# One Mish of 2048 columns per tile in place of an Exp-Ln-Exp chain per step, while attention runs

## Chip, core and metric

The kernel runs on one core of one Trainium2 chip. The metric is the device time of one launch in microseconds (us), as the median of several runs. A difference below 0.5% of this kernel's time (5.6 us) is called no change.

## What is computed

Causal attention with a decay, then two feed-forward layers on its output, all in float32:

```python
# B, H, S, D = 4, 8, 576, 64
scores = scale * np.matmul(q, k.transpose(0, 1, 3, 2))
decay = cum[:, :, :, None] - cum[:, :, None, :]
scores = np.where(causal, -1000000000.0, scores + decay)
attn = softmax(scores)                       # over the last axis
x = heads_joined(np.matmul(attn, v))         # 2304 tokens x 512
h = x @ w_in                                 # layer 1: 512 -> 2048
g = h * np.tanh(np.log1p(np.exp(h)))         # Mish
x = g @ w_out                                # 2048 -> 512
h = x @ moe2_w_in; g = h * np.cos(h); out = g @ moe2_w_out   # layer 2
```

## The kernel before

**Number format.** Matrix products run in float32r. To keep the accuracy every operand is split into a high and a low part (`gh`/`gl`, `wih`/`wil`, `woh`/`wol`), and a product is three matmuls: high times high, high times low, low times high.

**Attention** works on one pair of heads of one batch at a time, query block by query block (names `stk`, `s`, `mx`, `sm`, `p`, `xs`). PE makes the scores (L524), DVE adds the mask and takes the maximum (L560), ACT does the Exp (L565), DVE and POOL normalise (L576 to L579), PE transposes the probabilities (L606, L622), ACT and DVE copy them out of PSUM (L598, L600), and PE multiplies with v (L644). ACT and DVE split the result (L659, L660), and SP stores it to `xd` in DRAM.

**Layer 1 beside attention.** The first half of layer 1 (chunks 0 to 3 of eight, the "lo" weights) is done in tiles of 256 tokens. A tile is four steps of 512 columns: two blocks of 128 hidden units times 256 tokens, in one PSUM bank `h`. A step is 24 matmuls that make `h` (`mm_h`, L208), an activation, and 24 matmuls that bring the result back to 512 features in `acc` (`mm_o`, L230). Tiles are read from `xd` into `xa`. A tile is available when the whole batch that holds its last token is done, so layer 1 runs behind attention by about a batch, and its units are taken one by one between the pieces of attention, by a credit that is topped up at each piece. Tile 5 is held back (`LATE_TILES`) for the end of attention. `ffn_units` keeps three steps (`LAG = 3`) between the matmuls that make `h` and those that use the activated result.

**The activation** of a first-layer step is computed in two ways. When attention is over it is one ACTIVATE with the function Mish (L287). While attention runs, ACT uses a table of functions that holds Exp and Ln but not Mish, and the step is a chain: ACT Exp (L291), DVE twice (L302, L303), ACT Ln and Exp (L316, L317), DVE four times (L327 to L330, the last of which reads `h` from PSUM once more), ACT copy to `gh` (L338), POOL subtraction to `gl` (L344):

```python
nc.scalar.activation(out=e, in_=t, func=AF.Ln, bias=two)
nc.scalar.activation(out=e, in_=e, func=AF.Exp, scale=-1.0)
...
if n in hps and steps[n][1]["layer"] == 1:
    nc.gpsimd.tensor_tensor(out=gl, in0=st[n][0], in1=f(gst[n][0]), op=ALU.subtract)
```

**After attention** its PSUM banks and its SBUF pools (`att`) are given up, and new pools (`late`, `w1`) take their place. The rest of layer 1 follows (the other half of the weights, "hi", is first converted from a 64-bit layout by DVE, ACT and POOL, names `raw`, L123 to L138), then layer 2.

**Order.** The program is written unit by unit, and a scheduler then sets the order of the instructions on each engine. On the chip each engine works its list in that order.

Of the kernel before, what the change touches and what calls it, by code (L numbers as in the profile page):

```python
# [17 lines left out]
MISH_CAP = 485165195.40979  # L18
INV_2PI = 0.15915494309189535
TWO_PI = 6.283185307179586  # L20
ROUND = 12582912.0
# [15 lines left out]
def tile_attention_two_ffn(  # L37
# [35 lines left out]
    two = const.tile([128, 1], F32, name="two")  # L73
# [70 lines left out]
    def ffn_units(passes, p, hbank, abank, ready):  # L144
# [44 lines left out]
        def tmp(tag, n, dt=F32, bufs=3):  # L189
            tl = steps[n][1]  # L190
            t = p.tile([128, 512], dt, tag=tag, name=tag, bufs=bufs)
            return t[:, 0 : tl["G"] * tl["T"]]
# [103 lines left out]
        def v_1(n):  # L296
# [3 lines left out]
            t = tmp("n", n, F32, 2)  # L300
            if steps[n][1]["layer"] == 1:
                nc.vector.tensor_scalar(out=t, in0=e, scalar1=MISH_CAP, scalar2=2.0, op0=ALU.min, op1=ALU.add)  # L302
                marks["v1"] = nc.vector.scalar_tensor_tensor(  # L303
                    out=t, in0=e, scalar=MISH_CAP, in1=t, op0=ALU.min, op1=ALU.mult
                )
            else:
                nc.vector.tensor_scalar(out=t, in0=e, scalar1=ROUND, scalar2=ROUND, op0=ALU.add, op1=ALU.subtract)
                marks["v1"] = nc.vector.tensor_tensor(out=t, in0=e, in1=t, op=ALU.subtract)  # L308
            st[n].append(t)

        def a_mid(n):
            if n not in hps:
                return
            e, t = st[n]
            if steps[n][1]["layer"] == 1:
                nc.scalar.activation(out=e, in_=t, func=AF.Ln, bias=two)  # L316
                nc.scalar.activation(out=e, in_=e, func=AF.Exp, scale=-1.0)  # L317
            else:
                nc.scalar.activation(out=t, in_=t, func=AF.Sin, scale=TWO_PI)  # L319

        def v_2(n):
            e = st[n][0]
            if n in hps:
                t = st[n][1]
                if steps[n][1]["layer"] == 1:
                    r = tmp("r", n, F32, 1)
                    nc.vector.scalar_tensor_tensor(out=r, in0=t, scalar=2.0, in1=e, op0=ALU.add, op1=ALU.mult)  # L327
                    nc.vector.scalar_tensor_tensor(out=r, in0=r, scalar=2.0, in1=e, op0=ALU.subtract, op1=ALU.mult)
                    nc.vector.tensor_tensor(out=t, in0=t, in1=r, op=ALU.mult)
                    nc.vector.scalar_tensor_tensor(  # L330
                        out=e, in0=t, scalar=-UNSCALE, in1=hps[n], op0=ALU.mult, op1=ALU.mult
                    )
                else:
                    nc.vector.scalar_tensor_tensor(  # L334
                        out=e, in0=t, scalar=UNSCALE, in1=hps[n], op0=ALU.mult, op1=ALU.mult
                    )
# [4 lines left out]
        def v_3(n):  # L341
            gl = tmp("gl", n, F32R)
            if n in hps and steps[n][1]["layer"] == 1:
                nc.gpsimd.tensor_tensor(out=gl, in0=st[n][0], in1=f(gst[n][0]), op=ALU.subtract)  # L344
            else:
                marks["v1"] = nc.vector.tensor_tensor(out=gl, in0=st[n][0], in1=f(gst[n][0]), op=ALU.subtract)  # L346
# [3 lines left out]

        LAG = 3
        ok = lambda i: 0 <= i < N
        for m in range(N + LAG):
            if ok(m) and steps[m][3] == 0:
                while not ready(steps[m][0], steps[m][1]):
# [522 lines left out]
```

## Time and profile before

| what | value |
|---|---|
| median of 3 runs | 1125.5 us (1121.8 to 1126.73) |
| profiled execution | 1120.98 us, span 1119.2 us |
| PE busy | 1057.8 us, 95% |
| DVE busy | 692.5 us, 62% |
| ACT busy | 584.4 us, 52% |
| POOL busy | 274.3 us, 25% |
| attention's last matmuls, on the chain that ended last | 416.64 us, for 2.26 us |

Busy times are of one execution, from its first instruction. Up to about 60 us attention runs alone, from there to 420 us attention and the first tiles of layer 1 share the engines, and the rest is feed-forward work only. An engine that is idle costs time only where the others wait for it.

### The profile page before, as it was taken

To read this page: it belongs to the slowest core of one execution; us is meant where nothing else is said; L and a number is where in the kernel's file an instruction comes from. 1 tells how busy PE (TensorE), PEld (TensorE's weight loads), DVE (VectorE), ACT (ScalarE), POOL (GpSimd) and SP (SyncE) were. 2 spreads that over 40 slices of the span, in tenths; PEclk is the share of its full clock that TensorE was granted. 3 is DMA by queue.
4 is the path that set the end of the run, shared out by engine and by line. 5 is a ranking of instruction groups with operands and counts; after the bars stand their busy time and mean duration, and the time that the engine had idled before them with its cause. 6 is when DMAs were issued, how large, how long until landed. Compare 5 with 4: busy or idle time off the path is not lost.

```text
span 1119.2 us, 18191 instructions
## 1 busy us (share of the span) xinstructions
PE 1057.8 (95%) x6496; PEld 949.3 (85%) x6496; DVE 692.5 (62%) x1597; ACT 584.4 (52%) x1261; POOL 274.3 (25%) x365
## 2 busy tenths in 40 slices
PE   4688899889999999999999999999999999999998
PEld 3467688568877879999999999879999999999997
DVE  6888897668866764573456433996545454454543
ACT  5666777767765764454344433564434343343433
POOL 5557664434433421341111100231000000000000
PEclk9888999989998999999999999999999999999999
DMA  4635542251234102773555652641002020100000
GB/s 105 170 105 139 145 146 74 55 156 35 71 106 135 49 25 81 264 247 99 174 194 168 202 165 86 206 152 57 29 1 85 1 85 1 57 29 1 29 1 29
DMA packets 119503, 110.76 MB, mean 99 GB/s; under 512 B 65173, under 2 KB 101573, under 8 KB 119413
## 3 DMA queue, kind: packets, MB, share of 16 engines
q1 hardware_dynamic: 119412, 109.61, 31.8%
q8 instruction: 51, 0.84, 0.3%
q14 instruction: 40, 0.32, 0.1%
HBM read 81.12 MB, written 28.46 MB: 98 GB/s over the span
## 4 chain that ended last, share of the span: by engine, by line
PE 75%; DVE 10%; DMA 5%; issue 4%; ACT 4%; POOL 2%; SPq 1%; ACTq 0%; DVEq 0%; POOLq 0%
PE h L208 18%; PE acc L239 17%; PE acc L230 14%; PE hx L208 13%; PE s L644 4%; PE s L622 4%; PE s L524 3%; DMA raw<-in_moe_w_out_dram 3%; DVE s L560 2%; DVE stk L502 1%; DVE raw L133 1%; DVE raw L124 1%; PE s L482 1%; DMA xd<-xs 1%; ACT s L565 1%
## 5 line engine op out<-in xcount | busy, mean ns | idle before, releaser
L346 DVE TENSOR_TENSOR gl<-e,gh 128x384 fp32r<-128x384 f32 (+1 forms) x157 | 108.9, 695 | 131.7 <-ACT gh L338 131.0
L208 PE MATMUL hx<-x,wih 128*128 128x384 f32 (+1 forms) x640 | 160.3, 330 | 0.0
L208 PE MATMUL h<-x,wih 128*128 128x384 f32 (+1 forms) x640 | 158.6, 330 | 0.0
L338 ACT ACTIVATE gh<-e 128x384 fp32r<-128x384 f32 (+1 forms) x180 | 97.9, 545 | 101.4 <-DVE e L334 53.8
L230 PE MATMUL acc<-gh,woh 128*128 128x256 f32 (+1 forms) x480 | 147.5, 310 | 2.2 <-ACT part L267 1.7
L230 PE MATMUL acc<-gl,woh 128*128 128x256 f32 (+1 forms) x480 | 147.6, 308 | 0.9 <-POOL gl L344 0.9
L230 PE MATMUL acc<-gh,wol 128*128 128x256 f32 (+1 forms) x480 | 147.2, 307 | 0.0
L524 PE MATMUL s<-stk 68*128 68x192 f32 (+13 forms) x384 | 90.6, 343 | 31.7 <-DVE stk L502 19.0
L208 PEld LDWEIGHTS hx<-x,wih 128*128 128x128 f32 x640 | 115.1, 188 | 4.2
L208 PEld LDWEIGHTS h<-x,wih 128*128 128x128 f32 x640 | 115.1, 188 | 4.0
L579 POOL TENSOR_SCALAR s<-s,sm 128x448 f32<-128x448 f32 (+5 forms) x144 | 90.6, 642 | 108.4 <-DVE sm L577 59.3
L239 PE MATMUL acc<-woh,gl 128*128 128x512 f32 x288 | 113.3, 397 | 3.1 <-DVE gl L346 3.1
L239 PE MATMUL acc<-wol,gh 128*128 128x512 f32 x288 | 113.7, 395 | 0.0
L239 PE MATMUL acc<-woh,gh 128*128 128x512 f32 x288 | 112.3, 390 | 0.9 <-DVE part L275 0.9
L208 PE MATMUL h<-x,wil 128*128 128x384 f32 (+1 forms) x320 | 105.9, 331 | 0.0
L208 PE MATMUL hx<-x,wil 128*128 128x384 f32 (+1 forms) x320 | 105.8, 331 | 0.0
L524 PEld LDWEIGHTS s<-stk 128*128 128x128 f32 (+1 forms) x384 | 61.8, 206 | 44.6 <-DVE stk L502 15.6
L565 ACT ACTIVATE s<-s,mx 128x448 f32<-128x448 f32 (+5 forms) x144 | 83.3, 579 | 30.2 <-DVE mx L560 26.0
L319 ACT ACTIVATE n<-n 128x384 f32<-128x384 f32 x96 | 50.2, 523 | 92.4 <-DVE n L308 92.4
L230 PEld LDWEIGHTS acc<-gh,woh 128*128 128x128 f32 x480 | 91.7, 192 | 4.2 <-ACT part L267 2.2
L230 PEld LDWEIGHTS acc<-gl,woh 128*128 128x128 f32 x480 | 92.4, 193 | 1.5 <-POOL gl L344 1.1
L230 PEld LDWEIGHTS acc<-gh,wol 128*128 128x128 f32 x480 | 92.4, 193 | 0.1
(94 smaller groups left out, 2085.1 us busy)
## 6 DMA issues: line engine op xcount, KB each, us to landing
raw<-in_moe_w_in_dram SPq DMA_DIRECT2D x32, 512.0 KB
raw<-in_moe_w_out_dram SPq DMA_DIRECT2D x32, 512.0 KB
x<-xd SPq DMA_DIRECT2D x6, 1536.0 KB
x<-yd SPq DMA_DIRECT2D x6, 1536.0 KB
xd<-xs SPq DMA_DIRECT2D x12, 576.0 KB
xa<-xd SPq DMA_DIRECT2D x6, 1024.0 KB
natk<-in_k_dram SPq DMA_DIRECT2D x32, 144.0 KB
pd<-part SPq DMA_DIRECT2D x18, 256.0 KB
```

The costliest lines, as they stand in the source:

```text
L208: nc.tensor.matmul(o, lhsT=a[wsl], rhs=b[:, kk, :], start=(kk == 0 and i == 0), stop=(kk == NK - 1 and i == 2),)
L230: nc.tensor.matmul(o, lhsT=a[dsl], rhs=b[:, gs], start=(start and i == 0 and d % nsub == 0), stop=(end and i == 2), skip_group_check=True,)
L239: nc.tensor.matmul(acc[ti][m], lhsT=a[:, ms], rhs=b[:, j, :], start=(start and i == 0), stop=(end and i == 2),)
L319: nc.scalar.activation(out=t, in_=t, func=AF.Sin, scale=TWO_PI)
L338: nc.scalar.activation(out=gh, in_=e, func=AF.Copy)
L346: marks["v1"] = nc.vector.tensor_tensor(out=gl, in0=st[n][0], in1=f(gst[n][0]), op=ALU.subtract)
L524: marks["score"] = nc.tensor.matmul(o, lhsT=wide(st, rows, x, j, cols), rhs=st[rows, 1, x, j, c0:c1], start=x == 0, stop=x == 1,)
L560: marks["ttr"] = nc.vector.tensor_tensor_reduce(out=s[rs, c0:c1], in0=o[rs], in1=mk[rs], scale=-1.0, scalar=BIG if prev is None else prev, ...
L565: nc.scalar.activation(out=s[:, 0:w], in_=s[:, 0:w], func=AF.Exp, scale=-1.0, bias=mx, accum_out=sm[:, j : j + 1])
L579: nc.gpsimd.tensor_scalar(out=s[:, 0:w], in0=s[:, 0:w], scalar1=sm[:, j : j + 1], scalar2=1.0, op0=ALU.mult, op1=ALU.mult)
L622: nc.tensor.transpose(t[:, 128 * x : 128 * x + 128], ss[j][:, QS[c] : QS[c] + 128], ident)
L644: nc.tensor.matmul(t[64 * j : 64 * j + 64, c0:width], lhsT=vt[jb][0:kr, c, j], rhs=pt[0:kr, j, c, c0:width], start=(c == 0), stop=(c == nb ...
```

## The change

The chain is gone. While attention runs, layer 1 is now written by a generator `early()` that works tile by tile: it issues the 8 units of `mm_h` of a tile, and DVE copies each full bank of `h` out of PSUM with the scale applied, into one tile `hb` of 2048 columns. After the last of them one Mish of 2048 columns runs over `hb`, four ACT copies make the high part `ghb`, and four DVE subtractions the low part `glb`. The `mm_o` units of a tile come after the first three `mm_h` units of the next tile, if that one is available, and at once if not. `hb`, `ghb` and `glb` have one buffer each, in attention's SBUF pool. When attention is over, the `mm_o` units that are left are written out before the pools are closed, and the old generator goes on with the next tile (tile 6), whose input is now loaded into the `late` pool. The temporary tiles of the old generator move to that pool as well.

```diff
         def activate(n):
-            first_layer = steps[n][1]["layer"] == 1
             e = tmp("e", n)
-            if first_layer and attention_over:
+            if steps[n][1]["layer"] == 1:
                 nc.scalar.activation(out=e, in_=hps.pop(n), func=AF.Mish, scale=UNSCALE)
-                st[n] = [e]
-                return
-            if first_layer:
-                nc.scalar.activation(out=e, in_=hps[n], func=AF.Exp, scale=UNSCALE)
...
         def v_3(n):
             gl = tmp("gl", n, F32R)
-            if n in hps and steps[n][1]["layer"] == 1:
-                nc.gpsimd.tensor_tensor(out=gl, in0=st[n][0], in1=f(gst[n][0]), op=ALU.subtract)
-            else:
-                marks["v1"] = nc.vector.tensor_tensor(out=gl, in0=st[n][0], in1=f(gst[n][0]), op=ALU.subtract)
+            marks["v1"] = nc.vector.tensor_tensor(out=gl, in0=st[n][0], in1=f(gst[n][0]), op=ALU.subtract)
...
+        def early():
...
+                todo = [("o", n, jj) for n in own[prev] for jj in range(G)] if prev is not None else []
+                if go:
+                    todo[0:0] = [("h",) + u for u in units[0:3]]
+                    for x, u in enumerate(units[3:]):
+                        todo.insert(4 + 2 * x if prev is not None else 3 + x, ("h",) + u)
+                for kind, n, jj in todo:
+                    if kind == "h":
...
+                            nc.vector.tensor_scalar(
+                                out=parts[n - own[ti][0]], in0=hps.pop(n), scalar1=UNSCALE, scalar2=None, op0=ALU.mult
+                            )
...
+                if go:
+                    nc.scalar.activation(out=whole, in_=whole, func=AF.Mish)
...
+                        nc.scalar.activation(out=gh[:, sl], in_=parts[i], func=AF.Copy)
+                        nc.vector.tensor_tensor(out=gl[:, sl], in0=parts[i], in1=f(gh[:, sl]), op=ALU.subtract)
...
+    attention_done = True
+    while next(ffn) != "over":
+        pass
     att_ps.close()
     att_sb.close()
```

Three places of the program show how the instructions stand now. Lines of the changed kernel have other numbers: L551 scores, L592 Exp, L606 normalisation, L625 copies of p, L649 transposes, L671 products with v, L686 copy to xs, L206 `mm_h`, L228 `mm_o`, L366 Mish, L371 `ghb`, L168 loads of x.

ACT at tile 4, with all of the tile's `h` made in the rows before:

```order
L625 ACTIVATE p<-s_4384 128x2x2x128
L592 ACTIVATE s,sm<-s,mx 128x576
L366 ACT_TABLE_LOAD
L366 ACTIVATE hb<-hb 128x2048
L592 ACT_TABLE_LOAD
L592 ACTIVATE s,sm<-s,mx 128x64
```

The load of the functions' table stands ahead of the Mish, and a second one ahead of the next Exp. ACT has 13 such loads in the changed program, and 3 in the one before.

PE at the same place, from the row behind the last `mm_h` matmul of tile 4:

```order
L551 MATMUL s_4395<-stk_99 128x64
L649 MATMUL s_4418<-ident,s 128x128 x3
L649 MATMUL s_4423<-ident,s 128x128 x3
L551 MATMUL s_4432<-stk_99 128x192 x4
L671 MATMUL s_4445<-p,natv 64x320
L649 MATMUL s_4456<-ident,s 128x128 x4
L671 MATMUL s_4445<-p,natv 64x320
L671 MATMUL s_4445<-p,natv 64x256 x2
L671 MATMUL s_4445<-p,natv 64x128 x2
L649 MATMUL s_4462<-ident,s 128x128 x4
L551 MATMUL s_4486<-stk_99 128x320 x2
L551 MATMUL s_4489<-stk_99 128x320 x2
```

All of this is attention's. The scores `s_4489` are written into the bank from which ACT copies `s_4456` to p, and wait for that copy; ACT does it after the Mish, the second load and three Exps. Behind them come four transposes and tile 4's first `mm_o`.

ACT at the end of attention, where tile 5 has its Mish:

```order
L625 ACTIVATE p<-s_5031 128x4x128
L625 ACTIVATE p<-s_5037 128x4x128
L366 ACT_TABLE_LOAD
L366 ACTIVATE hb<-hb 128x2048
L686 ACTIVATE xs<-s_5008 128x320
L625 ACTIVATE p<-s_5068 128x4x128
L625 ACTIVATE p<-s_5074 128x4x128
L625 ACTIVATE p<-s_5080 128x2x128
L371 ACTIVATE ghb<-hb 128x512 x4
L686 ACTIVATE xs<-s_5097 128x256
```

The last three copies of p, for which attention's last products with v wait, stand behind the Mish. On PE those products come next, and after them all 96 `mm_o` matmuls of tile 5, with nothing else between; then the `mm_h` of tile 6.

SP at the hand-over, before (tile 6 is loaded into `xa`; names in brackets are the semaphores that an issue waits for):

```order
L664 DMA xd<-xs 256x1x576 [waits DMAHW6_49,DVE_49]
L170 DMA xa<-xd 128x8x256 [waits DMAHW6_49,DMAHW7_49,DMAHW5_49,DMAHW2_49]
L270 DMA pd<-part_5682 128x2x256 [waits DMAHW0_49,Activation_49]
L270 DMA pd<-part_5685 128x2x256 [waits DMAHW1_49,Activation_49]
L104 DMA raw<-in_moe_w_out_dram 128x1024 [waits DMAHW7_49,PE_49,Pool_49]
```

and in the changed kernel (tile 6 is loaded into `x`):

```order
L691 DMA xd<-xs 256x1x576 [waits DMAHW6_49,DVE_49]
L268 DMA pd<-part_5262 128x2x256 [waits DMAHW7_49,Activation_49]
L168 DMA x<-xd 128x8x256 [waits DMAHW2_49,DMAHW1_49,DMAHW5_49,DMAHW0_49,DMAHW6_49,PE_49,Pool_49]
L268 DMA pd<-part_5265 128x2x256 [waits Activation_49]
L102 DMA raw<-in_moe_w_out_dram 128x1024
```

The load of tile 6 now waits for PE, with the count of the last of tile 5's 96 `mm_o` matmuls; before it waited for other DMAs alone. The first load of a raw weight into the `late` pool waited for PE (the last `mm_h` of tile 6) before, and does no more.

## Rows read from the trace of the kernel before

**Rows 1.** The page's list of engines: busy us, share of the span, instructions.
```profile
PE 1057.8 (95%) x6496; PEld 949.3 (85%) x6496; DVE 692.5 (62%) x1597; ACT 584.4 (52%) x1261; POOL 274.3 (25%) x365
```

**Rows 2.** By stretch: length, PE, PEld, DVE, ACT, POOL busy, granted clock, DMA share, GB/s.
```profile
60.00:195.00 135.00, 122.52 (x921) 102.29 (x920) 114.37 (x316) 94.70 (x229) 82.01 (x106) 0.96 0.45 124
195.00:240.00 45.00, 39.89 (x250) 27.61 (x248) 28.18 (x113) 30.76 (x88) 18.20 (x37) 0.89 0.42 118
240.00:322.00 82.00, 79.99 (x626) 70.14 (x625) 63.75 (x182) 54.85 (x133) 35.47 (x52) 0.98 0.24 62
322.00:346.00 24.00, 21.73 (x134) 15.97 (x133) 13.01 (x48) 15.48 (x41) 7.43 (x15) 0.86 0.59 173
346.00:420.00 74.00, 71.90 (x552) 60.66 (x551) 54.18 (x158) 50.46 (x122) 28.52 (x41) 0.98 0.14 44
...
480.00:500.00 20.00, 18.23 (x134) 17.82 (x133) 15.42 (x21) 11.67 (x21) 8.40 (x6) 0.91 0.61 192
```

**Rows 3.** What PE waited for from 60 to 195 us: total us, times, longest.
```profile
PE s L622 <- DVE mx L560: 3.4, 4, 1.6
PE s L524 <- DVE mx L560: 1.7, 2, 1.3
...
PE acc L230 <- POOL gl L344: 0.9, 1, 0.9
```

**Rows 4.** All instructions on tile n, 60 to 430 us, by engine (DVE, then ACT).
```profile
60.00:430.00 370.00, 79.84 (x115) 16.57 (x23) 0.95 0.35 98
```

**Rows 5.** The chain's other groups, one shape each: count, busy us, mean ns, idle before.
```profile
L344 POOL TENSOR_TENSOR gl<-e,gh 128x512 fp32r<-128x512 f32 x23 | 31.1, 1351 | 29.2 <-ACT gh L338 28.5 <-POOL stk L508 0.7
...
L328 DVE SCALAR_TENSOR_TENSOR r<-r,e 128x512 f32<-128x512 f32 x23 | 17.2, 747 | 0.2
...
L317 ACT ACTIVATE e<-e 128x512 f32<-128x512 f32 x23 | 14.4, 625 | 0.3
...
L291 ACT ACTIVATE e<-h 128x512 f32<-128x512 f32 x23 | 13.6, 592 | 3.9 <-PE h L208 3.7
```

**Rows 6.** The same view: groups that are like what is added or stands near it.
```profile
L598 ACT ACTIVATE p<-s 128x512 f32<-128x512 f32 x80 | 46.2, 591 | 14.5 <-PE s L622 12.2 <-PE s L524 1.6
...
L338 ACT ACTIVATE gh<-e 128x512 fp32r<-128x512 f32 x36 | 22.5, 628 | 10.4 <-DVE e L330 5.1 <-PE acc L230 3.6 <-PE s L622 1.6
...
L287 ACT ACTIVATE e<-h 128x384 f32<-128x384 f32 x24 | 11.7, 486 | 14.0 <-PE h L208 13.8
...
L346 DVE TENSOR_TENSOR gl<-e,gh 128x512 fp32r<-128x512 f32 x13 | 11.4, 873 | 14.5 <-ACT gh L338 14.5
...
L565 ACT ACTIVATE s<-s,mx 128x192 f32<-128x192 f32 x24 | 10.7, 445 | 5.3 <-DVE mx L560 5.3
...
L287 ACT ACTIVATE e<-h 128x512 f32<-128x512 f32 x7 | 4.2, 597 | 1.5 <-PE h L208 1.5
...
L256 DVE TENSOR_SCALAR part<-acc 128x512 f32<-128x512 f32 x6 | 4.1, 684 | 3.9 <-PE acc L239 3.9
```

**Rows 7.** ACT's timeline at the first Mish: start us, us, instruction, idle before and its end.
```profile
425.57 1.28 ACT L287 ACT_TABLE_LOAD   x1 [0.28 <-PE h L208]
426.86 0.60 ACT L287 ACTIVATE e<-h 128x512 f32<-128x512 f32 x1
```

**Rows 8.** The chain that ended last, at the end of attention: start us, us, what.
```profile
412.40 1.24 PE s L622 x10
...
416.64 2.26 PE s L644 x18
...
423.13 5.34 DMA xa<-xd
428.47 0.14 issue
428.60 3.09 PE hx L208 x24
```

**Rows 9.** The same chain, 447 to 500 us, where the second half's weights are converted.
```profile
450.55 7.70 DMA raw<-in_moe_w_out_dram
```

More of the change, by code (lines that the diff above doesn't have):

```diff
@@ L72, in tile_attention_two_ffn @@
     maskt = const.tile([128, S], F32, name="maskt")
-    two = const.tile([128, 1], F32, name="two")
     quarter = const.tile([128, 1], F32, name="quarter")
@@ L190, in tmp @@
             tl = steps[n][1]
-            t = p.tile([128, 512], dt, tag=tag, name=tag, bufs=bufs)
+            t = late[0].tile([128, 512], dt, tag=tag, name=tag, bufs=bufs)
             return t[:, 0 : tl["G"] * tl["T"]]
@@ L299, in v_1 @@
             e = st[n][0]
[L300 to L305, printed above, removed]
-            else:
-                nc.vector.tensor_scalar(out=t, in0=e, scalar1=ROUND, scalar2=ROUND, op0=ALU.add, op1=ALU.subtract)
-                marks["v1"] = nc.vector.tensor_tensor(out=t, in0=e, in1=t, op=ALU.subtract)
+            t = tmp("n", n)
+            nc.vector.tensor_scalar(out=t, in0=e, scalar1=ROUND, scalar2=ROUND, op0=ALU.add, op1=ALU.subtract)
+            marks["v1"] = nc.vector.tensor_tensor(out=t, in0=e, in1=t, op=ALU.subtract)
             st[n].append(t)
@@ L313, in a_mid @@
                 return
[L314 to L319, printed above, removed]
+            t = st[n][1]
+            nc.scalar.activation(out=t, in_=t, func=AF.Sin, scale=TWO_PI)
         def v_2(n):
@@ L323, in v_2 @@
             if n in hps:
[L324 to L336, printed above, removed]
+                nc.vector.scalar_tensor_tensor(
+                    out=e, in0=st[n][1], scalar=UNSCALE, in1=hps[n], op0=ALU.mult, op1=ALU.mult
+                )
             gh = tmp("gh", n, F32R)
@@ L342, in v_3 @@
             gl = tmp("gl", n, F32R)
-            if n in hps and steps[n][1]["layer"] == 1:
-                nc.gpsimd.tensor_tensor(out=gl, in0=st[n][0], in1=f(gst[n][0]), op=ALU.subtract)
-            else:
-                marks["v1"] = nc.vector.tensor_tensor(out=gl, in0=st[n][0], in1=f(gst[n][0]), op=ALU.subtract)
+            marks["v1"] = nc.vector.tensor_tensor(out=gl, in0=st[n][0], in1=f(gst[n][0]), op=ALU.subtract)
             gst[n].append(gl)
@@ L351, in ffn_units @@
+        base = [0]
+        yield from early()
+        yield "over"
         LAG = 3
-        ok = lambda i: 0 <= i < N
-        for m in range(N + LAG):
+        ok = lambda i: base[0] <= i < N
+        for m in range(base[0], N + LAG):
             if ok(m) and steps[m][3] == 0:
-                while not ready(steps[m][0], steps[m][1]):
-                    yield None
                 load_x(steps[m][0])
@@ L359, in ffn_units @@
                 if ok(m):
-                    with ExitStack() as hold:
-                        if steps[m][0] in LATE_TILES:
-                            hold.enter_context(tc.issue_after(marks["score"].ins))
-                        mm_h(m, jj)
+                    mm_h(m, jj)
                     if jj == steps[m][1]["G"] - 1:
@@ L731, in tile_attention_two_ffn @@
     make_identity(nc, ident)
-    nc.gpsimd.memset(two, 2.0)
     nc.gpsimd.memset(quarter, 0.25)
@@ L800, in tile_attention_two_ffn @@
     w1a = weights = split_weights(1, lo, w0p)
-    done_tokens, attention_over, pos = 0, False, 0
+    done_tokens, attention_over, attention_done, pos = 0, False, False, 0
     psf, credit = None, 0.0
```

42 lines of the change are left out of this document (41 added, 1 removed).

## The prediction

> **What bounds the kernel now.** I read the page's engine list first, then the busy times by stretch, then what PE waits for, then the chain that ended last. PE is busy for 95% of the span, the others for two thirds or less [rows 1], and the change leaves PE its 6,496 matmuls. So whatever the change does must show as PE waiting less or more, or as a lower granted clock. The change touches the time from 60 to 420 us, where attention and layer 1 share the engines, and the hand-over behind it. The stretches [rows 2] are to be read by two numbers: the length less PE's busy time, and the granted clock. From 60 to 195 us (tiles 0 and 1) PE is idle for 12.5 us, and a clock of 0.96 costs at most 0.04 x 135 = 5.4 us. DVE is busy for 114.4 of these 135 us, 85%: this is the one stretch where DVE could be the limit. From 240 to 322 us (tiles 2 and 3) PE is idle for 2.0 us, and from 346 to 420 us (tiles 4 and 5) for 2.1 us, with a clock of 0.98 in both (1.6 and 1.5 us): there PE is the limit, with DVE at 78% and 73%. The two stretches between hold almost no layer 1; nothing changes in them. So however light the activation becomes, PE can win at most 12.5 + 5.4 + 2.0 + 1.6 + 2.1 + 1.5 = 25 us. The waits of the first stretch say whose part it is: most come from attention's maxima on DVE, which stand in DVE's queue among the chain's instructions (3.4 and 1.7 us in the two largest), and 0.9 us is the wait for POOL's `gl` [rows 3].
>
> **What is removed and added.** 23 steps lose six DVE operations each. Tile n is touched by five of them, 79.8 us together [rows 4], and L328 is 17.2 us [rows 5]: 97.0 us. ACT loses 16.6 [rows 4] + 14.4 + 13.6 us [rows 5] = 44.6, POOL 31.1 us of `gl` [rows 5]. Added on DVE for 24 steps: a copy of 512 columns out of PSUM, like L256 with 684 ns, 16.4 us, and `gl`, like L346 with 873 ns, 21.0 us [rows 6]. DVE is 60 us lighter. Added on ACT: a Mish of 384 columns takes 486 ns and one of 512 takes 597 [rows 6], that is 0.87 ns a column, so one of 2048 takes about 0.597 + 1536 x 0.00087 = 1.93 us, six of them 11.6 us; ten more table loads of 1.28 us [rows 7], 12.8 us; one more copy to `gh`. ACT is 20 us lighter. As sums of busy time all this is a gain, but none of these engines is the limit outside the first stretch.
>
> **What it gives.** Of the 17.9 us of the first stretch I give the change 8: the two waits for maxima (5.1), the 0.9 for `gl` and 2 of the clock. Of the 7.2 us of the other two I give it 2. The bounds are 3 us (a part of the first waits alone) and all 25.
>
> **What it costs: six waits behind a Mish.** The chain of before ran in pieces of less than a microsecond, three steps ahead of its use. Now all of a tile hangs on one sequence: last matmul of `h`, DVE copy 0.68, table load 1.28, Mish 1.93, with some 0.3 for a matmul's end and the hand-overs: 4.2 us. The load is inside it. At the first Mish of before ACT waited for PE's `h`, and only then the load began and took 1.28 us, with the Mish right behind [rows 7]. Everything that ACT has to do for attention stands behind this, and what follows first often needs the other table again, 1.28 us more. How much of it PE feels depends on the matmuls that stand in its list between the last `h` and the first instruction that needs something from behind the Mish. In the changed program these are 15, 22, 59, 62, 27 and 15 matmuls for tiles 0 to 5, at 0.124 to 0.129 us each [rows 8] (10 in 1.24, 18 in 2.26, 24 in 3.09): 1.9, 2.7, 7.3, 7.7, 3.3 and 1.9 us.
> Tile 4 as an example: Mish done at 4.2, load 1.28, three Exps of at most 0.445, copy to p 0.59 [rows 6]: 7.4 us. PE has work for 3.3, so it waits for 4.1, and for 0.6 more for the first `glb`. Tile 5: 4.2, a copy to xs that I put at 0.44 like the Exp, and three copies to p at 0.59 or a little less give 5.2, 5.8 and 6.4; PE has 1.9, then single matmuls, so it waits 3.9, then 0.4 for `glb`. Tile 0 (two short copies of attention, then `ghb` 0.63 and `glb` 0.87): 6.5 against 1.9 and two matmuls, 4.3. Tile 1 (a copy to p, then load, two Exps, `ghb`, `glb`): 4.1. Tiles 2 and 3 have attention or the next tile's `h` to do: 0 and 1.1. Together 18.5 us; PE's usual idle time in such stretches would have taken 2 or 3 of them anyway: I take 16. Bounds: 8, if the copies out of PSUM and ACT run ahead of what I assume, and 26, if DVE is busy when the last bank is full.
>
> **The hand-over.** Before, tile 6 was loaded while PE worked on tile 5: the load landed at 428.47 after 5.34 us, and its first matmul began with the issue behind it [rows 8]. Now that load waits for the last of tile 5's 96 `mm_o` matmuls, because it goes into memory that attention's pool held until then, and PE has nothing else to do. So 5.34 + 0.14 us stand open: 5.5, with 5 and 8 as bounds (a store of `pd` is issued just ahead of it). Against that the first weight of the second half is no longer held back until tile 6's `h` is made; before, its load of 7.70 us began only at 450.55 [rows 9], and the last of these weights made PE wait for 1.8 us between 480 and 500, where the clock of 0.91 cost another 20 x 0.09 = 1.8 [rows 2]. With loads that start some 20 us earlier against PE's work I take these 3.6 us as won (0 to 5).
>
> **The clock.** That stretch shows what follows a wait of 1.8 us: half speed for a while, 1.8 us lost. Five waits of 4 us or more would lose up to 9. I take 4, since in the first stretch PE is often at the low clock already; bounds 0 and 9. That a burst of `mm_o` with attention standing by (94 matmuls in one piece at tile 0) leaves less layer-1 work to fill attention's own gaps is in no term; it costs nothing as long as ACT and DVE have Exps and maxima to do meanwhile.
>
> **Sum.** -10 + 16 + 5.5 - 3.6 + 4 = +12 us on the profiled execution's 1121.0 us: 1133. That execution is 4.5 us below the median of the runs, 1125.5, so I forecast 1137 us, 1.0% slower.
>
> **A rule of the Trainium skill.** The row shows a load of 1.28 us whose Mish starts as it ends [rows 7]. The Trainium skill, "ScalarE: Activation LUTs", section "What ACT_TABLE_LOAD costs", puts a switch at about 2.66 us, since a drain of 1.38 us comes with the load; and its section "Table sets: the hidden batching unit" asks to batch calls by table set, which the old chain did (Exp and Ln in one set) and the new Mish between Exps does not. By that page the sum would hold 1.38 us more for each switch on PE's path. The trace shows no such drain, and the sum goes by the row.
>
> **The rivals.**
> *DVE was the limit after all* (faster). If maxima and copies come sooner everywhere, PE could take most of the 25 us, say 20, and with attention's chain ahead of PE the six waits shrink to their bound of 8: -20 + 8 + 5.5 - 3.6 + 2 = -8, 1117 us. For it speaks DVE's 85%; against it, that PE is 97% busy in two of the three stretches. It decides if the waits behind Mish come out below 12 us in sum. Chance 0.18.
> *Even* (within 0.5%, 1120 to 1131). The gain is 15 instead of 10, or the waits 10 instead of 16. Chance 0.22.
> *The forecast*, 1131 to 1145. Chance 0.45.
> *Switches cost more than the load.* If ACT has to empty itself ahead of a load that comes right behind a busy stretch, unlike the one row, each of the ten or so switches on PE's path costs as much again as the load itself, 1.28 us: +13, 1150 us. Against it: [rows 7]. Chance 0.15. This is the case of the page of the Trainium skill above, "ScalarE: Activation LUTs".
> That Mish needs no load at all is excluded by the order: 13 loads stand in the changed program.
>
> **Range and chances.** The low end takes in the even case and part of the first rival, the high end half of the last: 1118 to 1152. Faster 0.18, same 0.22, slower 0.60, with 0.5% (5.6 us) as what a measurement of this kernel can tell from no change.
>
> **What would show it.** In the changed profile: DVE about 60 us and ACT about 20 us less busy; Mish of 2048 columns near 1.93 us; ACT_TABLE_LOAD x13 at 1.28; PE waits of about 4 us before p or `ghb` at tiles 0, 1, 4 and 5 and almost none at 2 and 3; a wait of about 5.5 us before the first `hx` matmul, ended by the load of x; no wait for the weights 60 us later. I am wrong if attention ends more than 10 us earlier than at 419 us although 30 more layer-1 matmuls (3.7 us) now stand before its end, or if the waits at the Mish are filled by other work.

## The result and the profile after

The changed kernel takes 1138.3 us (median of 4 runs, 1137.7 to 1138.7) against 1123.8 us for the kernel before, run beside it: 1.0126 times as long, 95% interval 1.0099 to 1.0154. The forecast was 1137 us, slower, with its range from 1118 to 1152. The profiled execution has a span of 1135.9 us, 16.7 more than before. One of e10's twelve runs below took 2561 us and is in no ratio.

The page's list of engines, to be set against [rows 1]:

```profile
PE 1065.4 (94%) x6496; PEld 959.5 (84%) x6496; DVE 630.6 (56%) x1506; ACT 569.5 (50%) x1207; POOL 231.6 (20%) x341
```

The busy time by stretch, with the columns and the stretches of [rows 2]:

```profile
60.00:195.00 135.00, 117.36 (x816) 98.52 (x815) 89.75 (x261) 82.97 (x191) 62.05 (x90) 0.85 0.40 109
195.00:240.00 45.00, 41.31 (x273) 30.52 (x271) 28.47 (x107) 31.43 (x86) 17.11 (x35) 0.89 0.32 83
240.00:322.00 82.00, 80.81 (x627) 70.80 (x628) 47.00 (x157) 53.91 (x124) 22.00 (x45) 0.96 0.31 87
...
346.00:420.00 74.00, 71.46 (x525) 61.42 (x524) 39.22 (x140) 43.05 (x107) 20.11 (x40) 0.91 0.24 71
480.00:500.00 20.00, 20.00 (x169) 20.00 (x168) 9.38 (x16) 9.93 (x17) 4.22 (x4) 1.00 0.50 158
```

DVE is 62 us lighter, ACT 15 and POOL 43, and the kernel is slower: the engines that were relieved were not the limit. The 16.7 us split cleanly. The same 6,496 matmuls keep PE busy 7.6 us longer (1065.4 against 1057.8), which goes with a lower granted clock (0.960 against 0.977 over the whole span). PE is idle 9.1 us more (1135.9 - 1065.4 = 70.5 against 61.4).

Where it is lost is seen by following the layer-1 matmuls (`mm_h` and `mm_o`) by their number, a count that is the same in both programs. Tiles 0 and 1 end with the 384th, tiles 2 and 3 with the 768th. That count alone does not say how much of attention is done by then, so three more points follow: the start of attention's 720th and 1290th matmul, by which every program has done the same attention and exactly 384 and 768 layer-1 matmuls, and of PE's 2752nd matmul, ahead of which all 1600 matmuls of attention and 1152 of layer 1 are done. Start in us, of the profiled executions (e1 and so on are the experiments below):

| kernel | 384th | 768th | 1026th | attention 720th | attention 1290th | PE 2752nd | span |
|---|---|---|---|---|---|---|---|
| before | 190.0 | 324.1 | 416.4 | 197.7 | 340.4 | 434.3 | 1119.2 |
| after | 204.5 | 329.2 | 420.8 | 211.2 | 351.2 | 445.6 | 1135.9 |
| e1 chain left out | 191.3 | 318.1 | 411.0 | 198.0 | 339.4 | 429.2 | 1112.7 |
| e2 Mish by step | 204.8 | 333.7 | 430.1 | 211.5 | 354.7 | 448.8 | 1131.9 |
| e3 Exp for Mish | 198.0 | 323.6 | 411.3 | 204.7 | 346.0 | 435.6 | 1125.9 |
| e4 tile 6 early | 204.5 | 328.1 | 420.2 | 211.2 | 350.0 | 445.1 | 1131.8 |
| e5 input weights first | 200.1 | 323.9 | 413.5 | 203.1 | 347.0 | 438.4 | 1129.3 |
| e7 own memory | 203.1 | 328.8 | 421.2 | 209.8 | 350.5 | 446.0 | 1127.2 |
| e8 e5 and e7 | 199.8 | 322.1 | 413.7 | 202.8 | 344.8 | 438.6 | 1119.9 |
| e9 hybrid | 189.9 | 317.8 | 415.9 | 197.9 | 339.0 | 442.0 | 1123.1 |
| e10 hybrid, no empty turns | 196.2 | 324.5 | 413.2 | 204.2 | 345.1 | 437.2 | 1118.4 |
| e11 two tiles | 192.0 | 324.6 | 422.0 | 199.7 | 345.9 | 440.8 | 1121.8 |
| e12 before, own memory | 189.9 | 325.1 | 416.5 | 197.6 | 342.3 | 434.8 | 1116.2 |

After against before, by the layer-1 count: 14.5 us lost up to the 384th, 9.4 won back by the 768th, and from the 1026th to the end 715.1 us instead of 702.8, 12.3 lost. But this compares unequal work. Ahead of the 768th stand 1204 matmuls of attention in the kernel before and in e12, 1182 in e1, e2 and e9 to e11, 1172 in the changed kernel, e3, e4 and e7, and 1168 in e5 and e8; the rest is done behind it. By the points of equal work the change loses 13.5 us up to attention's 720th, wins 2.7 between its 720th and its 1290th, loses 0.6 from there to PE's 2752nd, loses 9.2 in the 48 matmuls behind that (14.9 instead of 5.7 us), and wins 3.9 later. So most of the 9.4 us is a change of order and no gain. The kernel before and e12 have the same PE list up to there and differ by 2.0 us between attention's 720th and 1290th (142.7 and 144.8), so 2.7 is hardly more than two executions differ by.

**The first loss** has two halves. Up to 133 us, counted by line, 96 `mm_h` matmuls and no `mm_o` were run from 60 us on; the kernel before did 80 and 72. So attention had less layer-1 work to fill its gaps with, PE was busy for 59.8 of 73 us (65.0 before), and the clock was 0.85 (0.92 before):

```profile
60.00:133.00 73.00, 59.83 (x409) 46.96 (x407) 54.59 (x158) 44.57 (x112) 46.14 (x63) 0.85 0.51 136
```

The chain of this stretch shows what tile 0 waited for, and what came when it was ready (start, us, what):

```profile
99.20 5.48 DMA raw<-in_moe_w_in_dram
...
127.11 3.80 DMA raw<-in_moe_w_out_dram
...
133.30 1.28 ACT L366
134.59 1.92 ACT hb L366
...
139.39 13.22 PE acc L228 x94
```

By tile, all `mm_h` stand ahead of the first `mm_o`, and so need the input weights of all four chunks; these were loaded and converted chunk by chunk, each with its output weights, which nobody used before 138 us. Then 94 `mm_o` come in one piece.

By 133 us PE has done 59 matmuls fewer than before, and up to 195 us it falls back by another 48. In this other half PE is busy for as long as before, at a lower clock. The rows, with the columns of [rows 2], are of the kernel before, the changed one, and e3, which has its order but no switches:

```profile
133.00:195.00 62.00, 57.56 (x455) 50.21 (x454) 52.59 (x148) 44.30 (x107) 32.12 (x46) 1.00 0.44 124
```

```profile
133.00:195.00 62.00, 57.53 (x407) 51.56 (x408) 35.16 (x104) 38.40 (x80) 15.91 (x28) 0.86 0.27 77
```

```profile
133.00:195.00 62.00, 59.63 (x460) 53.30 (x461) 38.40 (x116) 37.22 (x88) 17.74 (x32) 0.94 0.27 78
```

In the changed kernel the clock is at its low level, half, from 133.5 to 143.7 and from 181.2 to 188.1 us, around and behind the Mishes of tiles 0 and 1 (134.6 and 177.5); in e3 only from 133.1 to 140.0, and in the kernel before not at all.

**The last loss** is the hand-over (the chain again):

```profile
434.33 11.60 PE acc L228 x96
445.93 6.67 issue
452.60 5.37 PE hx L206 x24
```

PE is idle for 6.7 us behind tile 5's `mm_o`, while tile 6 is loaded (the load is issued at 446.47); the next 24 matmuls take 5.37 instead of 2.88 us, 2.5 more.

**The Mish** itself is as forecast, the groups by line:

```profile
L366 ACT ACTIVATE hb<-hb 128x2048 f32<-128x2048 f32 x6 | 11.5, 1913 | 0.2
...
L366 ACT ACT_TABLE_LOAD x6 | 7.7, 1283 | 2.4 <-DVE hb L356 2.3
```

### The profile page after: what moved, and what is told of

Its sections match the earlier page's. It is cut to its first block, busy times and chain, and to the rows that moved or that the text cites. A ratio compares the mean times of both kernels' runs of the same rounds, so it can differ in the third digit from the quotient of the medians.

```text
span 1135.9 us, 17924 instructions
## 1 busy us (share of the span) xinstructions
PE 1065.4 (94%) x6496; PEld 959.5 (84%) x6496; DVE 630.6 (56%) x1506; ACT 569.5 (50%) x1207; POOL 231.6 (20%) x341
## 4 chain that ended last, share of the span: by engine, by line
PE 80%; DVE 8%; ACT 5%; issue 3%; DMA 2%; POOL 1%; ACTq 0%; DVEq 0%; POOLq 0%
PE h L206 19%; PE acc L228 17%; PE acc L237 16%; PE hx L206 14%; PE s L671 4%; PE s L551 4%; PE s L649 4%; DVE s L587 1%; DVE stk L529 1%; PE s L509 1%; ACT s L592 1%; DVE raw L122 1%; DVE raw L131 1%; DVE raw L121 1%; DMA raw<-in_moe_w_in_dram 1%
## 5 line engine op out<-in xcount | busy, mean ns | idle before, releaser
L206 PE MATMUL hx<-x,wih 128*128 128x384 f32 (+1 forms) x672 | 168.4, 331 | 6.7 <-issue 6.7
L206 PE MATMUL h<-x,wih 128*128 128x384 f32 (+1 forms) x672 | 164.4, 328 | 0.0
L206 PEld LDWEIGHTS hx<-x,wih 128*128 128x128 f32 x672 | 121.9, 192 | 11.1 <-issue 6.9
L311 ACT ACTIVATE gh<-e 128x384 fp32r<-128x384 f32 (+1 forms) x156 | 82.9, 531 | 95.9 <-DVE e L307 54.1
L551 PE MATMUL s<-stk 68*128 68x192 f32 (+13 forms) x384 | 95.0, 358 | 35.9 <-DVE stk L529 20.1
L206 PEld LDWEIGHTS h<-x,wih 128*128 128x128 f32 x672 | 120.1, 188 | 4.0
L606 POOL TENSOR_SCALAR s<-s,sm 128x448 f32<-128x448 f32 (+5 forms) x144 | 83.0, 590 | 171.0 <-DVE sm L604 73.9
L206 PE MATMUL hx<-x,wil 128*128 128x384 f32 (+1 forms) x336 | 111.3, 331 | 0.0
L206 PE MATMUL h<-x,wil 128*128 128x384 f32 (+1 forms) x336 | 110.4, 329 | 0.0
L551 PEld LDWEIGHTS s<-stk 128*128 128x128 f32 (+1 forms) x384 | 66.9, 222 | 46.8 <-DVE stk L529 14.5
L592 ACT ACTIVATE s<-s,mx 128x448 f32<-128x448 f32 (+5 forms) x144 | 83.5, 580 | 36.5 <-DVE mx L587 33.0
L228 PE MATMUL acc<-gh,wol 128*128 128x384 f32 (+1 forms) x288 | 91.3, 317 | 0.0
L228 PE MATMUL acc<-gl,woh 128*128 128x384 f32 (+1 forms) x288 | 91.3, 317 | 0.0
L228 PE MATMUL acc<-gh,woh 128*128 128x384 f32 (+1 forms) x288 | 91.3, 317 | 0.0
L587 DVE CUSTOM_DVE_ANT_0 s<-s,maskt 128x384 f32<-128x384 f32 (+7 forms) x160 | 70.7, 454 | 36.8 <-PE s L551 30.7
L671 PE MATMUL s<-p,natv 128*64 128x256 f32 (+5 forms) x544 | 78.0, 389 | 4.5 <-ACT p L625 2.6
L206 PE MATMUL h<-xa,wih 128*128 128x256 f32 x384 | 80.2, 297 | 1.4 <-ACT wih L135 1.4
```

Source lines behind the costliest of these rows:

```text
L206: nc.tensor.matmul(o, lhsT=a[wsl], rhs=b[:, kk, :], start=(kk == 0 and i == 0), stop=(kk == NK - 1 and i == 2),)
L228: nc.tensor.matmul(o, lhsT=a[dsl], rhs=b[:, gs], start=(start and i == 0 and d % nsub == 0), stop=(end and i == 2), skip_group_check=True,)
L311: nc.scalar.activation(out=gh, in_=e, func=AF.Copy)
L551: marks["score"] = nc.tensor.matmul(o, lhsT=wide(st, rows, x, j, cols), rhs=st[rows, 1, x, j, c0:c1], start=x == 0, stop=x == 1,)
L587: marks["ttr"] = nc.vector.tensor_tensor_reduce(out=s[rs, c0:c1], in0=o[rs], in1=mk[rs], scale=-1.0, scalar=BIG if prev is None else prev, ...
L592: nc.scalar.activation(out=s[:, 0:w], in_=s[:, 0:w], func=AF.Exp, scale=-1.0, bias=mx, accum_out=sm[:, j : j + 1])
```

## The experiments

The theory after the trace (T): the order by tile starves the first stretch, the hand-over costs 9 us, and the lighter chain gives little. Its rivals: the table loads are what costs (R1), and a lighter chain gives PE much more than it seems (R2). All ratios below are to the kernel before, run on the same chip in the same series; the changed kernel's 1.0126 has a series of its own and an interval of about 0.28% to each side, so differences to it are known to some 0.35%, 4 us.

**e1: the chain left out, old order.** The kernel before, with one Exp in place of the chain (the output is that of Exp, not Mish), and `gl` on DVE.

```diff
-            if first_layer and attention_over:
-                nc.scalar.activation(out=e, in_=hps.pop(n), func=AF.Mish, scale=UNSCALE)
+            if first_layer:
+                fn = AF.Mish if attention_over else AF.Exp
+                nc.scalar.activation(out=e, in_=hps.pop(n), func=fn, scale=UNSCALE)
```

> The kernel before, with its order of steps, but in attention a first-layer step's activation is one Exp of 512 columns instead of the chain, then the copy to gh and the subtraction for gl on DVE; the Mish is left out there, and no table load is added. My theory (PE can win only what it waits for in the first stretch, term of 10 us): 5 to 12 us faster than the kernel before, 1112 to 1119 us. Rival (DVE was the limit): 20 us or more faster, below 1105 us.

Measured: 0.9921 (0.9897 to 0.9946), some 9 us less. R2 falls: a chain at almost no cost, with no switch, is worth less than 1%. The stretches are instructive:

```profile
60.00:195.00 135.00, 125.88 (x919) 106.03 (x917) 90.09 (x275) 85.94 (x213) 66.73 (x98) 0.90 0.45 122
240.00:322.00 82.00, 82.00 (x663) 73.32 (x662) 41.31 (x145) 48.83 (x125) 22.02 (x46) 1.00 0.26 69
```

With DVE at 90 instead of 114 us, PE's idle time in the first stretch fell from 12.5 to 9.1 us, but the clock went from 0.96 to 0.90, and the 384th matmul came no earlier. From 240 to 322 us, where I had seen PE as the limit, nothing is left of PE's idle time and low clock. By the points of equal work e1 loses 0.3 us up to attention's 720th, wins 1.3 up to its 1290th and 4.0 from there to PE's 2752nd.

**e2: the same order, Mish by step,** with a switch of tables at each step (39 loads).

```diff
-            if first_layer and attention_over:
+            if first_layer:
```

> The same as the run with the chain left out, and with the same order on PE, but the activation is the Mish, step by step: 39 table loads in place of 3, 46 us more of loads on ACT. My theory (loads hurt only where PE has nothing else to do, since three steps lie between a step's activation and its use): 5 to 15 us slower than the run with the chain left out. Rival (the loads are what made the change slow): 30 us or more slower than it.

Measured: 1.0144 (1.0114 to 1.0173). Against e1 that is 2.2%, 25 us, for 36 more loads: 0.7 us for a load that takes 1.28. T had put this too low, R1 too high.

**e3: the changed kernel's order, Exp for the Mish** (same size, 1.91 us; 3 loads; the output is that of Exp).

```diff
-                    nc.scalar.activation(out=whole, in_=whole, func=AF.Mish)
+                    nc.scalar.activation(out=whole, in_=whole, func=AF.Exp)
```

> The changed kernel with its order on PE, but with an Exp of 2048 columns in place of the Mish (Mish left out in attention), so that no table is switched: 3 loads in place of 13. My theory: of the waits behind the Mish, 8 to 11 us in the trace, the loads are about a third: 3 to 6 us faster than the changed kernel, 1132 to 1135 us. Rival (the loads are what made it slow): 12 us or more faster, 1126 or less.

Measured: 1.0061 (1.004 to 1.0082), 0.65% or 7 us below the changed kernel: ten loads at 0.7 us, as in e2. It is still slower than the kernel before without a single switch more. So the loads are about half of the loss, and the order makes the rest: against e1, nearly the same work in the old order, e3 is 1.4% (16 us) longer. In the traces 6.7 us of that lie ahead of attention's 720th matmul and 9.2 at the hand-over, which e3 leaves as it was.

**e4: tile 6 loaded before tile 5's last `mm_o`,** into attention's memory as in the kernel before.

```diff
                 for kind, n, jj in todo:
+                    if attention_done:
+                        load_x(ti)
                     if kind == "h":
```

> The changed kernel, but the input of tile 6 is loaded into attention's pool as before, ahead of tile 5's last matmuls, so that the load waits for attention's store alone. My theory: the wait of 6.7 us at the hand-over and the low clock behind it (2.5 us) go, and up to 3.6 us come back at the second half's weights, whose first load waits for tile 6 again: 5 to 9 us faster than the changed kernel, 1129 to 1133 us. Rival (attention's store is the real wait): 0 to 2 us faster.

Measured: 1.0104 (1.008 to 1.0128), 2 to 4 us less than the changed kernel, between what T and its rival expected. The chain says why:

```profile
445.37 2.85 PE hx L206 x24
...
453.92 2.85 PE h L206 x24
...
456.85 0.66 ACT wih L135
457.51 0.97 ACT e L284 x2
...
460.13 0.84 DVE gl L316
...
461.01 4.68 PE acc L228 x25
```

The wait for x is gone, and a new one of 4.2 us stands in its place: `wih` of the second half is written only when tile 6's last `mm_h` is done (456.78), and tile 6's first Mishes stand behind it in ACT's list. That `wih` lies in memory that `xa` held was then a guess, and e7 puts it to the test.

**e5: input weights first.** The first half's weights are converted in another order: all input pieces, then all output pieces; `mm_h` waits for the former alone.

```diff
+        if layer == 1 and c_first(chunks):
+            todo = [(s_, c, which) for which in "io" for s_, c in enumerate(chunks)]
...
-            while (tl["layer"], c) not in converted:
+            need = (1, c, "i") if tl["layer"] == 1 and c < C1 else (tl["layer"], c)
+            while need not in converted:
                 next(weights)
```

> The changed kernel, with the first half's layer-1 weights converted in another order: first the input pieces of all four chunks, then the output pieces, so that the mm_h of tile 0 wait for the input pieces alone. Theory after the first four runs: without table loads the order by tile alone made the 384th layer-1 matmul come 6.5 us later than the order by step (198.0 against 191.3 us), because tile 0's mm_h trickle behind weights that its mm_o do not need yet; then 4 to 8 us of the changed kernel's loss go away here, the 384th layer-1 matmul comes at 197 to 201 instead of 204.5 us, and the ratio to the kernel before falls from 1.0126 to 1.006 to 1.009. Rival: what costs is the lump of tile 0's 94 mm_o with attention standing by, which is as long as before; then at most 2 us go away (ratio above 1.010).

Measured: 1.0066 (1.0046 to 1.0087), 0.6% or 7 us less than the changed kernel, the 384th matmul at 200.1, attention's 720th 8.1 us earlier. By 133 us PE is busy for 64.0 us with 450 matmuls (59.8 and 409 in the changed kernel):

```profile
60.00:133.00 73.00, 64.02 (x450) 50.23 (x449) 49.05 (x151) 48.25 (x114) 37.69 (x55) 0.86 0.39 100
```

**e7: tile 6 early, in memory of its own.** As e4, with `xa` of even tiles outside attention's pool.

```diff
-                t = ap.tile([128, 2, NK, TA], F32R, tag="xa", name="xa", bufs=2)
+                t = (ap if ti % 2 else p).tile([128, 2, NK, TA], F32R, tag="xa", name="xa", bufs=1)
```

> The changed kernel, with tile 6 loaded ahead of tile 5's last mm_o as in the run before, but into memory that neither attention's pool nor the second half's weights use (one of the two buffers of xa is kept outside attention's pool; a temporary of layer 2 has two buffers instead of three). Theory: the hand-over costs 6.7 us of wait for the load of x and some 2.5 us of low clock behind it; the run with the early load alone gave only 4 us of that back, because the memory of xa was then what the second half's weights waited for. With memory of its own both waits go: 8 to 13 us less than the changed kernel, the time from the 1026th layer-1 matmul to the end falls from 715 to 702 to 706 us, ratio to the kernel before 1.001 to 1.006. Rival: the conversion of the second half's weights is late whatever memory it uses, and the same wait of some 4 us stays in front of tile 6's first mm_o; then 3 to 5 us less, ratio 1.008 to 1.010.

Measured: 1.0061 (1.0039 to 1.0082), 7 us less than the changed kernel; from the 1026th matmul to the end 706.0 instead of 715.1 us. No wait is left at the hand-over:

```profile
434.74 11.58 PE acc L228 x96
446.32 2.86 PE hx L206 x24
```

So it was the memory of `xa` that made e4's second wait, and the hand-over's price is 7 to 9 us.

**e8: e5 and e7 together.**

> Both of the edits above (input weights first, tile 6 in memory of its own). If the two losses are separate, as the theory has it, the gains add: 12 to 20 us less than the changed kernel, ratio to the kernel before 0.995 to 1.002; what stays of the loss is the table loads and the waits behind the Mish. If one of the two was only a wait in front of another, the sum falls short of the two by 3 us or more.

Measured: 0.9981 (0.9964 to 0.9999), 1.45% or 16 us below the changed kernel. The two gains (0.6 and 0.65%) add, within the 0.35%, so these were separate losses. With both repaired, the change is even with the kernel before.

**e9: a hybrid.** The chain by step for tiles 0 and 1, then one Mish by tile for tiles 2 to 5, tile 6 as in e7.

```diff
-        yield from early()
+        yield from chain_units(1)
+        yield from early()
```

(`chain_units` is the old generator cut to two tiles, `early` begins at tile 2.)

> Tiles 0 and 1 as in the kernel before (Exp-Ln-Exp chain by step, no table load), tiles 2 to 5 by tile with one Mish, and tile 6 in memory of its own. Theory: the first stretch, where the changed kernel lost 13 us, runs as before (384th layer-1 matmul at 189 to 193 us); the stretch of tiles 2 and 3 keeps the changed kernel's gain (384th to 768th layer-1 matmul in 123 to 129 us instead of 134); tiles 4 and 5 lose 3 to 5 us at their Mishes; the hand-over costs nothing. Together 1110 to 1117 us, ratio to the kernel before 0.990 to 0.998. Rival: the switch of tables and the order by tile cost their price wherever they are, and the later stretches only seemed to gain because they had been delayed; then the ratio is 1.000 or more.

Measured: 1.0032 (1.0013 to 1.0051): missed. The first stretch (189.9) and tiles 2 and 3 (127.9 us from the 384th to the 768th) came as expected, though 22 matmuls of attention fewer stand ahead of that 768th and the gain between attention's 720th and 1290th is 1.6 us; the end did not:

```profile
419.12 2.24 PE s L747 x18
421.36 1.63 PE h L208 x12
...
423.01 0.70 DVE hb L432
...
423.74 1.92 ACT hb L442
...
426.87 0.53 ACT ghb L447
...
427.41 0.83 DVE glb L448
...
428.29 13.95 PE acc L230 x94
```

Tile 5's last `mm_h` came behind attention's last product. Nothing was left on PE to cover its Mish: 5.3 us pass from the end of `mm_h` to the 94 `mm_o`, which then take 13.95 us instead of 11.6.

**e10: the hybrid without three empty turns** at the chain's end, which had used up the credit of later units.

```diff
-                    yield m
+                    if ok(m):
+                        yield m
```

> The hybrid of the run before (chain for tiles 0 and 1, one Mish for tiles 2 to 5), with three empty turns taken out of the chain's end, so that tile 5's mm_h come before attention's last products and its Mish has work of PE behind it. Theory: the hybrid lost 7.8 us behind attention's end, since its tile 5 got its Mish when PE had nothing left but that tile's 96 mm_o (a wait of 4.5 us, then 94 matmuls in 13.95 instead of 11.6 us). Then 4 to 7 us of that go away: ratio to the kernel before 0.997 to 1.000. Rival: the wait only moves to attention's last products, as in the changed kernel, where it was 2 us and more; then at most 3 us go away, ratio above 1.000.

Measured: 0.9952 (0.993 to 0.9974), 0.8% below e9, more than expected. Tile 5's `mm_h` now end ahead of attention's last 20 products, which cover its Mish: PE waits 1.4 us for `ghb`, and the 94 `mm_o` run at full clock. The chain:

```profile
421.15 1.28 ACT L443
...
422.45 1.91 ACT hb L443
...
424.53 0.63 ACT ghb L448
...
425.93 11.55 PE acc L230 x94
437.48 2.88 PE hx L208 x24
```

**e11: one Mish for tiles 2 and 3 alone,** the chain elsewhere, `xa` as in e12, and a preload of the chain's table after the second Mish.

```diff
+        yield from in_steps(0, first)
+        yield from by_tile(2, 3)
+        with tc.issue_after(marks["mish"].ins):
+            nc.scalar.preload_act_table_set("natural_log_exp_and_others")
+        yield from in_steps(last, N)
```

> The kernel before, with one Mish by tile for tiles 2 and 3 alone (two Mishes, five table loads and one preload in all), the chain by step for tiles 0, 1, 4, 5 and 6, and the memory of xa as in the run beside it. Theory: a Mish by tile pays where PE has other work in its list for as long as copy, load, Mish and second load take (tiles 2 and 3, where the changed kernel and both variants gained 4 to 6 us between the 384th and the 768th layer-1 matmul) and costs where it has not. Then the 384th to 768th layer-1 matmul take 124 to 130 us instead of 134, nothing is lost before or after, and with the weights' 3.8 us the kernel takes 7 to 10 us less than the one before: ratio 0.991 to 0.994, the fastest of the study that computes everything. Rival: the gain of tiles 2 and 3 came from lighter engines in the tiles around them; then only the weights' 3 to 4 us stay: 0.996 to 0.998.

Measured: 1.0000 (0.9979 to 1.0021), 0.34% slower than e12, which has its memory and no Mish: the theory missed, and its rival too. From the 384th to the 768th matmul it took 132.6 us (e12: 135.2), and then lost 6 us up to the 1026th; but 22 matmuls of attention fewer stand ahead of its 768th. By the points of equal work it gained nowhere: it is 2.1 us behind e12 at attention's 720th, 3.6 at its 1290th and 6.0 at PE's 2752nd. One place is seen on ACT's timeline at tile 3:

```profile
298.44 1.92 ACT L399 ACTIVATE store<-store 128x2048 f32<-128x2048 f32 x1
300.38 1.28 ACT L453 ACT_TABLE_LOAD   x1
301.68 0.60 ACT L668 ACTIVATE p<-s 128x512 f32<-128x512 f32 x1
302.17 0.55 ACT L635 ACTIVATE s<-s,mx 128x320 f32<-128x320 f32 x1
...
302.71 1.66 ACT L403 ACTIVATE gh<-store 128x512 fp32r<-128x512 f32 x3
304.27 0.85 ACT L668 ACTIVATE p<-s 128x512 f32<-128x512 f32 x2
```

The copies of p for which PE waits stand behind the preload and three copies to `gh`; PE waits 1.9 us for them. In e9 a copy of p comes right behind the Mish, ahead of the load. The rest of its loss is not explained.

**e12: the kernel before with the memory of e7,** and nothing of the change (behind the hand-over the temporary r takes the memory of `part1`).

> The kernel before, with one of the two buffers of xa kept outside attention's pool and the small temporary r moved into that pool; nothing else. It asks for the term of the second half's weights alone: in every kernel of this study that converts these weights without waiting for tile 6's mm_h, the stretch from 460 to 545 us had no wait, and took 3.8 us less than the kernel before. If that is all that holds them back, this kernel is 3 to 5 us faster than the kernel before: ratio 0.9955 to 0.9975. If the memory of xa is not what the load waited for, nothing changes: 0.999 to 1.001.

Measured: 0.9966 (0.9944 to 0.9987), 3.8 us less, and no wait is left where the weights of the second half made one [rows 2]:

```profile
480.00:500.00 20.00, 20.00 (x164) 20.00 (x163) 15.83 (x18) 10.99 (x19) 7.78 (x6) 1.00 0.67 217
```

## Why the prediction came out as it did

The total was right, and partly by luck. By the points of equal work the first stretch was wrong by some 18 us (13.5 lost, 3.7 of them in waits around a Mish, where 8 were to be won). The other way, the waits were 8 us too many, and the later stretches won some 4 us more than forecast, their waits aside. In the profiled executions 16.7 us were lost where the sum has 12.

- **"-10: what it gives"** failed in its main place. I gave 8 us of it to the first stretch, and that stretch lost 13.5 us. The step that failed is the last sentence of "The clock": that layer-1 work in one burst "leaves less layer-1 work to fill attention's own gaps is in no term; it costs nothing as long as ACT and DVE have Exps and maxima to do". It cost about 7 us by e5, since a tile of `mm_h` needs all four chunks' input weights; the loads are another part (204.5 against 198.0 us for the 384th matmul, e3), in the half behind 133 us. And no gain was seen to be had: e1 relieved DVE as much, and in its one profiled execution the stretch came no earlier.
- The 2 us of the other two stretches were somewhat low. The changed kernel won 2.7 us with tiles 2 and 3, where no wait stands against it, and lost 0.6 with tiles 4 and 5, where 3.9 us of waits do; e1, with no switch, won 1.3 and 4.0. I had called PE the limit there; yet at 97% and a clock of 0.98 [rows 2] the waits and the clock together left 3.6 us in 240 to 322 us alone, and e1 has none of them.
- **"+16: six waits behind a Mish"** were too many by half: 1.9, 1.9, 0, 0, 2.5 and 1.4 us for tiles 0 to 5, 7.6 in sum, of PE's idle time around and behind the Mish; 1.3 of it (0.7 at tile 1, 0.6 at tile 4) are waits for maxima and copies of DVE, which do not stand behind the Mish. Tiles 2 and 3 are free, nearly as forecast (0 and 1.1). At tile 4 the sequence on ACT came out as worked out: PE's last `mm_h` ends at 374.04, and the scores that wait for the copy to p start at 381.30, 7.3 us later (forecast 7.4). ACT's timeline, then PE's:

```profile
374.73 0.19 ACT L592 ACTIVATION_READ_ACCUMULATOR s<-s,mx 128x1 f32 x1
374.93 1.28 ACT L366 ACT_TABLE_LOAD   x1
376.23 1.91 ACT L366 ACTIVATE hb<-hb 128x2048 f32<-128x2048 f32 x1
378.15 1.28 ACT L592 ACT_TABLE_LOAD   x1
```

```profile
373.77 0.27 PE L206 MATMUL h<-xa,wil 128*128 128x256 f32 x1
...
378.95 0.54 PE L551 MATMUL s<-stk 128*128 128x320 f32 x2
381.30 0.56 PE L551 MATMUL s<-stk 128*128 128x320 f32 x2 [1.81 <-ACT p L625]
```

  What was off is the work of PE in between: it lasted until 379.5, 5.4 us with a wait of 0.6 for a copy of p by DVE, where I had counted matmuls at full pace for 3.3. In the trace 33 matmuls stand there and not 27, at tile 5 20 and not 15: the products with v run for each of the two heads, and the list as I read it shows them once; and those of 320 columns take longer than 0.129 us. At tile 5 the load also ran beside DVE's last copy of `h` (427.47 and 427.46), so the Mish was done 3.3 us behind the last `mm_h` and not 4.2; at tile 1 the load came behind that copy. The wait at tile 4 is short, but the low clock behind it is not: 0.58 from 382 to 386 us.
- **"+5.5: the hand-over"** was the right mechanism at the wrong size: 6.7 us of wait and 2.5 of clock behind it, and 7 us came back in e7.
- **"-3.6: the second half's weights"** was right, in place and in size, as e12 shows by itself (3.8 us).
- **"+4: the clock"** was too low: the same matmuls keep PE busy 7.6 us longer, and this is after the gain at 480 to 500 us. I had taken 4 and not 9 since "in the first stretch PE is often at the low clock already", against my own row of 0.96 [rows 2]; there was much to lose, and from 133 to 195 us the clock fell from 1.00 to 0.86.
- **The rivals.** *DVE was the limit after all* falls with e1: 9 us for the whole chain, and none seen in the first stretch. *Switches cost more than the load* falls as it was put: the rows above show, at tile 4, a load behind a busy ACT, within 0.02 us of the end of the instruction ahead of it, and the Mish within 0.02 us of the load's end. "ScalarE: Activation LUTs" of the Trainium skill, "What ACT_TABLE_LOAD costs", has a drain of 1.38 us there; the trace shows none here either. What the section "Table sets: the hidden batching unit" of that page of the Trainium skill asks for does agree: 36 switches more cost 25 us in e2.

**What adds up.** Loads with the waits they make 7.3 us (e3), the order of the weights 6.7 (e5), the hand-over 7.3 (e7): 21.3, if all three add as the last two do (e8). The change lost 14.2 (1.26% of 1123.8), so it won some 7, and 3.8 of these are the weights of the second half, which need no change of the activation (e12). Each of the three is known to some 4 us only, but the traces say the same: 3.9 us won with the weights and 2.7 with tiles 2 and 3.

What stays open: most of e11's loss, and whether the change wins anything with tiles 2 and 3. The gain from the 384th to the 768th matmul is for the most part only put off: e9 won 6.2 us there against the kernel before and gave back 5.8 by the 1026th, with 22 matmuls of attention moved from the one stretch to the other. That the loads' share of the first loss is the low clock behind 133 us, and the weights' share the time before, is read from one execution of each kernel; no run has both edits. e10 against e12 (0.9952 and 0.9966, intervals that overlap) says that a Mish by tile behind a chain for the first two tiles is worth nothing that can be measured.

## What to carry to other kernels

Before work is regrouped into larger pieces, list what the first piece needs that it did not need before (here all four chunks of weights instead of one) and what filled the other engine's gaps until then: that cost as much as the table switches did. To find where a change loses time, compare the programs at points by which both have done the same work of every kind; a count of one kind alone shows a change of order as a gain. A pool that is closed at a change of phase ties the next phase's first load to the last reader of its memory; a buffer of its own was worth 0.3% without any other change and 0.65% with this one. A switch of tables is best priced by a kernel that only adds switches: 0.7 us each here, half of what a load takes.

## What was not expected of the hardware

The granted clock of a stretch differs between programs that are the same up to there. e9 and e10 have the same instructions in the same order on every engine up to 195 us, and this is a stretch of e9, and below it the same of e10:

```profile
75.00:95.00 20.00, 15.24 (x112) 11.02 (x113) 18.28 (x51) 14.79 (x37) 12.28 (x14) 1.00 0.42 113
```

```profile
75.00:95.00 20.00, 18.38 (x95) 13.36 (x95) 15.59 (x41) 13.04 (x31) 10.34 (x13) 0.66 0.41 113
```

Clock 1.00 in the one and 0.66 in the other, with 112 and 95 matmuls done, and the 384th layer-1 matmul at 189.9 and 196.2 us. So a difference of 6 us in the first stretch of two single executions says nothing by itself: that e5 and e3 gain at all is carried by their medians (6.7 and 7.3 us), where they gain is read from one execution each, and that e1 gains nothing there is not shown to better than these 6 us. The five programs that have the first stretch of the kernel before gave 190.0, 189.9, 189.9, 192.0 and 196.2, the three that have that of the changed kernel 204.5, 204.5 and 203.1: that difference repeats. And a relieved DVE did not help there in e1's one trace: with PE's idle time down by 3.4 us, the clock was lower by 0.06.
